# Weight conversion interleaved with the first queries and the first two pairs, in one PSUM rotation

## The chip, the core and the metric

The kernel runs on one core of a Trainium2 chip. Times are device microseconds (us) of one execution; the figure of a kernel is the median of its runs, and less is better.

## What is computed

Attention with a memory, followed by a two-layer feed-forward net, all in float32. Batch 4, 8 heads, 576 tokens, 64 features per head; 2304 tokens in all, 512 features, 2048 hidden features. Of the reference:

```
scores = scale * q @ k^T, causal, softmaxed over keys
local  = a @ v
q_p    = where(q > 0, q, exp(q) - 1) + 1
mem    = (q_p @ M_prev) / (q_p . z_prev + 1e-6)
out    = g * mem + (1 - g) * local          # g = sigmoid(beta), per head
x      = out as (tokens, 512)
h      = x @ w_in
y      = (h * sigmoid(1.702 * h)) @ w_out
```

## The kernel before

Matmuls run on pairs of 32-bit parts: every operand is split in a high part and a low remainder, and three products (high by high, low by high, high by low) are added in PSUM. The weights come as raw 64-bit words. `conv_unit` turns a block of them (128 hidden features) into the two parts in five steps: `load` (a 512 KB transfer into one of two raw buffers `wraw`), `scale` (ScalarE writes `ws` into a PSUM bank), `bits` (three VectorE passes, L177, L178 and L180, the last one giving `wr` and reading both the raw words and `ws`), a copy of the high part `wi` on ScalarE, and the subtraction of the low part on GpSimd. There are 16 blocks of w_in. "Load n" and "conversion n" below are those of the n-th block, in the order in which they are issued.

Attention goes by pairs of heads: pair p is batch p // 4, heads 2 (p % 4) and one more. `plan_prep` places a pair's preparation in numbered slots: `split_hi` on ScalarE, `split_lo_k` and `split_lo_q` on GpSimd, `stack_hi` and `stack_lo` (ten SBUF-to-SBUF transfers, which put high and low parts of keys and queries above each other in `W`), the phi function of the queries and its normalisation. `plan_attend` places the scores (`s_unit`, tiles `ps`), row maxima on VectorE (L483), exponentials on ScalarE (L489), row scaling on GpSimd (L492), transposes (`pt`), their split (`e`) and the products with the values (`po`). Pair p + 1 begins 7 or 8 slots after pair p.

The first 256 tokens of batch 0 are done ahead of that by `first_queries`, all four pairs of heads at once and with their own tiles (`fk`, `fq`, `fa`, ...), so that the first token chunk `x` is there early. `first_moe` is a generator of the matmuls of x @ w_in (tiles `pm`, one block of w_in after another for each chunk of tokens); `step` runs a slot's events and then takes matmuls from this generator up to the slot's share of TensorE time (`PACE`). The results `hk` go out to `gd`. When the attention of a batch is complete (`xd`), its next chunks follow. The second product (tiles `acc`) comes after all of it.

The program's order is a wish list: the framework's scheduler orders each engine's instructions at build time by it, by its own estimate of times, and puts in the waits. On the chip each engine, and the transfer queue of SyncE (SP), issues in that order. A tile from a pool waits for the release of the buffer that it takes over.

PSUM has eight banks: two for `pm`, one for `po`, and five for scores, transposes and conversion: a rotation of four (`ps_s`) and a single one (`ps_x`). The conversions use `ps_x`; after the slot of the last conversion, each fifth tile of attention takes it. All six conversions of the first group (`W0`) are written after `first_queries`, then the loads of pair 0, then the slots from -7 on, with the ten other conversions at the slots of `CONV`.

Of the kernel before, what the change touches and what calls it, by code (L numbers as in the profile page):

```python
# [8 lines left out]
F32 = mybir.dt.float32  # L9
# [25 lines left out]
def tile_attention_memory_moe(ctx, tc, kq, vq, mem, zz, beta, w_in, w_out, out):  # L35
# [5 lines left out]
    PACE = ((20, 2.2), (60, 2.2), (9999, 2.7))  # L41
    LATE = 20
    W0 = 6
    CONV = [-7, -6, -5, -3, -1, 1, 3, 5, 7, 9]
    PSUM = bass.MemoryType.PSUM

    def pool(stack, name, bufs=1, **kw):
        return stack.enter_context(tc.tile_pool(name=name, bufs=bufs, **kw))
# [12 lines left out]
    att = pool(attn, "att", side="right")  # L61
    wkp = pool(attn, "wkp", side="right")
    sml = pool(attn, "sml", 6, side="right")
    ps_s = pool(attn, "ps_s", 4, space=PSUM, side="right")
    ps_x = pool(attn, "ps_x", 1, space=PSUM, side="right")
    ps_o = pool(attn, "ps_o", 1, space=PSUM, side="right")

    xd = [dr.tile([128, NK, S], F32, name=f"xd{b}") for b in range(B)]
# [1 line left out]

    moe_ps = [(ps_m, "pm")]
    events = {}
    state = {"slot": -8, "pe": 0.0, "seq": 0, "sum": 0, "bank": 0}


    def bank(name):
        state["bank"] += 1
        own = state["slot"] > CONV[-1] + 1 and state["bank"] % 5 == 4
        return (ps_x if own else ps_s).tile([128, 512], F32, name=name, tag="ps")

    def at(slot, prio, fn):
        assert slot > state["slot"], (slot, state["slot"])
# [129 lines left out]
    def first_queries(b):  # L212
        K, fsm = [], []
        if b == 0:
            nc.sync.dma_start(gb, beta.to_broadcast([128, H]))
        for c in range(NP):
            t = fst.tile([128, 512], F32, name=f"fk{c}")
            nc.sync.dma_start(t[:, :256], kq[b, c, :, :256])
            nc.sync.dma_start(t[:, 256:], kq[b, c, :, S:S + 256])
            K.append(t)  # L220
        q = fst.tile([128, NP, 2, 128], F32, name="fq")
        nc.sync.dma_start(q, vq[b, :, :, 1, :2].rearrange("c p t d -> p c t d"))
        z = fst.tile([128, NP, 128], F32, name="fz")
        nc.sync.dma_start(z.rearrange("p c d -> p (c d)"), zz[b:b + 1].rearrange("o c d -> o (c d)").to_broadcast([128, NP * 128]))
        v = fst.tile([128, NP, 2, 128], F32, name="fv")
        nc.sync.dma_start(v, vq[b, :, :, 0, :2].rearrange("c p t d -> p c t d"))
        m = fst.tile([128, NP, 128], F32, name="fm")
        nc.sync.dma_start(m, mem[b * NP:b * NP + NP].rearrange("c p h d -> p c (h d)"))
        qm = fst.tile([128, NP * 2, 2, D + 1], F32, name="fqm")
        nc.gpsimd.memset(qm[:, :, :, D:], 1e-6)  # L230
        for c in range(NP):
            fs = fst.tile([128, 2, 2, 2], F32, name="fsm", bufs=NP)
            nc.gpsimd.memset(fs, 1e-9)
            fsm.append(fs)
        box = {}
        aa, fa = {}, {}

        def score(c):
            ps = []
            for h in range(2):  # L240
                r = slice(64 * h, 64 * h + 64)
                p = bank("ps")
                nc.tensor.matmul(p[:, :256], K[c][r, 384:512], K[c][r, :256], start=True, stop=True)
                nc.tensor.matmul(p[:, 256:384], K[c][r, 256:384], K[c][r, :128], start=True, stop=True)
                ps.append(p)
            aa[c] = fst.tile([128, 2, 384], F32, name="fa", bufs=2)
            for h in range(2):
                for i, (o, n) in enumerate(((256, 128), (0, 256))):
                    nm = softmax_max([(ps[h][:, o:o + n], n, mask[:, 512 - n:])])
                    softmax_exp(ps[h][:, o:o + n], aa[c][:, h, o:o + n], nm, fsm[c][:, h, i, :1])  # L250

        def norm(c):
            sm = fst.tile([128, 2, 2], F32, name="fsr", bufs=2)
            nc.vector.tensor_reduce(out=sm, in_=fsm[c], op=ALU.add, axis=AX.X)
            nc.vector.reciprocal(out=sm, in_=sm)
            for h in range(2):
                for i, (o, n) in enumerate(((256, 128), (0, 256))):
                    scale_rows(aa[c][:, h, o:o + n], sm[:, h, i:i + 1], g1[:, 2 * c + h:2 * c + h + 1])
            pt = [bank("pt") for _ in range(2)]
            for h in range(2):  # L260
                nc.tensor.transpose(pt[0][:, 256 * h:256 * h + 128], aa[c][:, h, 256:384], ident)
                nc.tensor.transpose(pt[0][:, 256 * h + 128:256 * h + 256], aa[c][:, h, 0:128], ident)
                nc.tensor.transpose(pt[1][:, 128 * h:128 * h + 128], aa[c][:, h, 128:256], ident)
            fa[c] = fst.tile([128, 768], F32, name="ft", bufs=2)
            copy("A", fa[c][:, :512], pt[0])
            copy("V", fa[c][:, 512:], pt[1][:, :256])

        def phi():
            qv = q.rearrange("p c t (h d) -> p (c t) h d", h=2)
            w = qm[:, :, :, :D]  # L270
            nc.scalar.activation(out=w, in_=qv, func=AF.Relu, scale=-1.0)
            nc.scalar.activation(out=w, in_=w, func=AF.Exp, scale=-1.0)
            nc.vector.scalar_tensor_tensor(out=qv, in0=qv, scalar=0.0, in1=w, op0=ALU.max, op1=ALU.add)
            for c in range(NP):
                tt("P", w[:, 2 * c:2 * c + 2], qv[:, 2 * c:2 * c + 2],
                   z[:, c:c + 1, :].rearrange("p o (h d) -> p o h d", h=2).to_broadcast([128, 2, 2, D]), ALU.mult)
                copy("A", m[:, c], m[:, c], gt[:, c:c + 1])

        def phin():
            n = fst.tile([128, NP, 2, 2, 1], F32, name="fn")  # L280
            nv = n.rearrange("p c t h o -> p (c t) h o")
            nc.vector.tensor_reduce(out=nv[:, :, :, 0], in_=qm, op=ALU.add, axis=AX.X)
            nc.vector.reciprocal(out=n, in_=n)
            for c in range(NP):
                w = q[:, c].rearrange("p t (h d) -> p t h d", h=2)
                tt("P", w, w, n[:, c].to_broadcast([128, 2, 2, D]), ALU.mult)

        def qtr(k):
            if not k:
                box["qt"] = fst.tile([128, NP, 256], F32, name="fqt")  # L290
            qt = box["qt"]
            pt = bank("pt")
            for c in (2 * k, 2 * k + 1):
                for t in range(2):
                    o = 128 * (2 * (c % 2) + t)
                    nc.tensor.transpose(pt[:, o:o + 128], q[:, c, t], ident)
            copy("A", qt[:, 2 * k:2 * k + 2].rearrange("p c q -> p (c q)"), pt)

        def values(c, xl):
            for h in range(2):  # L300
                r = slice(64 * h, 64 * h + 64)
                po = (ps_o if h == 0 else ps_m).tile([128, 512], F32, name="po" if h == 0 else "pm")
                nc.tensor.matmul(po[:, :256], m[:, c], box["qt"][:, c], start=True, stop=False)
                nc.tensor.matmul(po[:, :256], v[:, c, 0], fa[c][:, 256 * h:256 * h + 256], start=False, stop=False)
                nc.tensor.matmul(
                    po[:, 128:256], v[:, c, 1], fa[c][:, 512 + 128 * h:640 + 128 * h], start=False, stop=True)
                copy("A", xq[b][0][r, c, :256], po[r, :256])
                sub("V", xl[r, c, :256], po[r, :256], xq[b][0][r, c, :256])

        if b == 0:  # L310
            gates()
        xl = new_x(b)
        xq[b][0] = mop.tile([128, NK, XW], F32R, name="xh")
        score(0)
        phi()
        score(1)
        norm(0)
        phin()
        score(2)
        norm(1)  # L320
        qtr(0)
        qtr(1)
        values(0, xl)
        score(3)
        norm(2)
        values(1, xl)
        norm(3)
        values(2, xl)
        values(3, xl)

# [397 lines left out]
    NPAIRS = len(pairs)  # L728
    def conv_in(blk):
        wb[blk] = w1[blk >= W0].tile([128, 2, DM], F32R, name=f"wi{blk}")  # L730
        conv_unit(None, wb[blk], w_in[blk], cnv, {"bufs": 2}, lambda: ps_x, {"tag": "ps"}, att, {"tag": f"qpt{blk % 2}", "bufs": 2})

    for b in range(MB):
        first_queries(b)
        xplan[b] = -7
        if b == 0:
            for blk in range(W0):
                conv_in(blk)
    first.close()
    w1.append(pool(left, "w1b", side="left", reuse_waits="tile"))  # L740
    load_kq(0)
    load_vq(0)
    for p in range(NPAIRS):
# [1 line left out]
        plan_attend(p)  # L745
    for blk in range(W0, NB):
        at(CONV[blk - W0], 58, lambda blk=blk: conv_in(blk))
    fill["gen"] = first_moe()
    while state["slot"] < K0[-1] + 16:
        step()  # L750
# [134 lines left out]
```

## Time and profile before

| | us |
|---|---|
| median of 3 runs | 687.38 (687.28 to 688.12) |
| the profiled execution | 689.67 |
| its span, first to last instruction | 687.8 |
| TensorE busy in it | 631.3 |
| VectorE busy | 442.4 |
| ScalarE busy | 406.9 |
| GpSimd busy | 277.9 |

PE is TensorE, DVE VectorE, ACT ScalarE, POOL GpSimd, SPq the queue of SyncE, from which all transfers are issued. PEclk is the granted clock of TensorE as a share of its full speed. In a row of the timeline stand its start, its duration, engine, line, operation, result <- sources, the shape and the count of merged instructions, and in brackets the idle time of the engine ahead of it and what ended it. A transfer's duration there is the time of its issue, not of its bytes.

### The profile page before, as it was taken

What the parts mean: (1) busy time and instruction counts of PE and PEld (TensorE: products, weight loads), DVE (VectorE), ACT (ScalarE), POOL (GpSimd) and SP (SyncE); (2) the same over time, 40 slices, a digit from 0 to 9 for tenths busy, and PEclk for the clock granted to TensorE, in tenths of its full rate; (3) what the DMA queues carried; (4) which work ended last, traced back from release to release, by engine and by line L of the source; (5) the groups of instructions that cost most, each with busy time, mean ns of one, the idle gap of its engine ahead of it and who ended that gap; (6) DMA issues with size and microseconds to landing.
All of it is one profiled execution on the core that took longest, in us unless ns stands there. A gap on an engine that the chain in (4) does not pass through costs nothing.

```text
span 687.8 us, 12522 instructions
## 1 busy us (share of the span) xinstructions
PE 631.3 (92%) x3984; PEld 574.7 (84%) x3984; DVE 442.4 (64%) x1128; ACT 406.9 (59%) x988; POOL 277.9 (40%) x319
## 2 busy tenths in 40 slices
PE   4687788789998799999899998999999999999997
PEld 3476777579986699999899997999888888888897
DVE  3887678857758776687658634826865545555453
ACT  5766478867748785777576534514555445454453
POOL 4967377776637694566485202422500000000000
PEclk9989899999999999999999999999999999999999
DMA  7869548877667666766772127946544335344231
GB/s 257 248 172 276 177 134 233 244 202 189 176 181 195 183 202 186 194 191 172 230 207 77 45 79 262 321 145 229 153 117 133 118 103 157 92 127 134 67 126 55
DMA packets 71427, 116.71 MB, mean 170 GB/s; under 512 B 8769, under 2 KB 41025, under 8 KB 71361
## 3 DMA queue, kind: packets, MB, share of 16 engines
q1 hardware_dynamic: 71360, 115.91, 57.6%
q8 instruction: 32, 0.52, 0.3%
q14 instruction: 35, 0.28, 0.1%
HBM read 63.97 MB, written 27.79 MB: 133 GB/s over the span
## 4 chain that ended last, share of the span: by engine, by line
PE 71%; DMA 8%; DVE 8%; ACT 6%; issue 2%; SPq 2%; POOL 2%; DVEq 0%; ACTq 0%; POOLq 0%
PE acc L89 29%; PE pm L89 25%; PE po L89 6%; PE pt L93 5%; PE ps L89 5%; DMA qr<-in_vq_dram 2%; DMA xl<-xd 2%; DMA kqr<-in_kq_dram 1%; DVE ps L483 1%; DVE e L108 1%; DMA gd<-hk 1%; ACT a L489 1%; ACT hi L98 1%; ACT e L98 1%; DMA wraw<-in_w_in_dram 1%
## 5 line engine op out<-in xcount | busy, mean ns | idle before, releaser
L89 PE MATMUL pm<-xh,wi 128*128 128x288 f32 (+2 forms) x1024 | 224.5, 308 | 15.3 <-ACT hk L98 5.5
L89 PEld LDWEIGHTS pm<-xh,wi 128*128 128x128 f32 x1024 | 170.7, 195 | 19.3 <-ACT hk L98 6.1
L89 PE MATMUL acc<-gh,wo 128*128 128x512 f32 (+1 forms) x640 | 179.3, 368 | 0.0
L89 PE MATMUL pm<-xl,wi 128*128 128x288 f32 (+2 forms) x512 | 155.7, 305 | 0.0
L89 PEld LDWEIGHTS acc<-gh,wo 128*128 128x128 f32 x640 | 115.2, 189 | 19.8
L89 PE MATMUL acc<-gl,wo 128*128 128x512 f32 (+1 forms) x320 | 115.1, 368 | 0.0
L89 PEld LDWEIGHTS pm<-xl,wi 128*128 128x128 f32 x512 | 99.7, 195 | 0.4
L492 POOL TENSOR_SCALAR a<-a,sm,g 128x512 f32<-128x512 f32 (+3 forms) x112 | 71.9, 653 | 65.3 <-DVE sm L531 43.6
L108 DVE TENSOR_TENSOR e<-pt,e 128x320 fp32r<-128x320 f32 (+2 forms) x152 | 70.1, 482 | 39.1 <-ACT e L98 38.3
L785 DVE SCALAR_TENSOR_TENSOR gt<-gt,graw 128x512 f32<-128x512 f32 (+1 forms) x80 | 53.0, 662 | 45.6 <-ACT gt L784 45.1
L483 DVE CUSTOM_DVE_ANT_0 ps<-ps,mask 128x256 f32<-128x256 f32 (+4 forms) x144 | 69.7, 494 | 19.2 <-PE ps L89 14.1
L784 ACT ACTIVATE gt<-graw 128x512 f32<-128x512 f32 (+1 forms) x80 | 47.2, 591 | 55.6 <-DVE gl L108 55.6
L108 DVE TENSOR_TENSOR gl<-gt,gh 128x512 fp32r<-128x512 f32 (+1 forms) x80 | 53.1, 665 | 36.3 <-ACT gh L98 33.2
L489 ACT ACTIVATE a<-ps,nm 128x512 f32<-128x512 f32 (+3 forms) x112 | 60.7, 544 | 26.7 <-DVE nm L483 25.7
L89 PE MATMUL po<-e,vs 128*128 128x320 f32 (+3 forms) x416 | 71.6, 292 | 4.6 <-ACT e L98 4.1
L98 ACT ACTIVATE e<-pt 128x320 fp32r<-128x320 f32 (+2 forms) x152 | 62.2, 436 | 22.4 <-PE po L89 11.5
L98 ACT ACTIVATE gh<-gt 128x512 fp32r<-128x512 f32 (+1 forms) x80 | 47.2, 590 | 41.0 <-PE acc L89 38.6
L89 PEld LDWEIGHTS acc<-gl,wo 128*128 128x128 f32 x320 | 59.4, 189 | 10.1
L89 PEld LDWEIGHTS po<-e,vs 128*128 128x128 f32 x416 | 62.1, 191 | 6.4 <-ACT e L98 4.9
L89 PE MATMUL ps<-W 128*128 128x512 f32 (+3 forms) x224 | 59.9, 350 | 4.4 <-DVE e L108 2.9
L93 PE MATMUL pt<-ident,a 128*128 128x128 f32 x296 | 57.4, 276 | 0.4 <-ACT a L489 0.3
L98 ACT ACTIVATE hk<-pm 128x288 f32<-128x288 f32 (+2 forms) x64 | 26.2, 409 | 53.1 <-PE pm L89 43.7
(125 smaller groups left out, 979.2 us busy)
## 6 DMA issues: line engine op xcount, KB each, us to landing
graw<-gd SPq DMA_DIRECT2D x64, 256.0 KB, 2.7
gd<-hk SPq DMA_DIRECT2D x96, 144.0 KB, 2.6
wraw<-in_w_in_dram SPq DMA_DIRECT2D x16, 512.0 KB, 4.3
wraw<-in_w_out_dram SPq DMA_DIRECT2D x16, 512.0 KB, 5.0
kqr<-in_kq_dram SPq DMA_DIRECT2D x12, 608.0 KB, 5.2
W<-hi SPq DMA_DIRECT2D x24, 272.0 KB, 3.8
W<-loq SPq DMA_DIRECT2D x48, 128.0 KB, 3.7
vr<-in_vq_dram SPq DMA_DIRECT2D x16, 320.0 KB, 4.3
```

The costliest lines, as they stand in the source:

```text
L89: nc.tensor.matmul(out, l, r, start=start, stop=stop)
L93: nc.tensor.transpose(out, in_, idn)
L98: nc.scalar.activation(out=dst, in_=src, func=AF.Copy, **kw)
L108: (nc.vector if eng == "V" else nc.gpsimd).tensor_tensor(out=dst, in0=a, in1=b, op=op)
L483: nc.vector.tensor_tensor_reduce(out=ps, in0=ps, in1=mk, op0=ALU.add, op1=ALU.min, scale=-0.125, scalar=1e38 if j == 0 else nm[:, j - 1:j] ...
L489: nc.scalar.activation(out=a, in_=ps, func=AF.Exp, scale=-1.0, bias=nm, accum_out=sm)
L492: nc.gpsimd.tensor_scalar(out=a, in0=a, scalar1=r, scalar2=gcol, op0=ALU.mult, op1=ALU.mult)
L784: nc.scalar.activation(out=t[:, :n], in_=raw[:, :n], func=AF.Tanh, scale=0.851)
L785: nc.vector.scalar_tensor_tensor(out=t[:, :n], in0=t[:, :n], scalar=1.0, in1=raw[:, :n], op0=ALU.add, op1=ALU.mult)
```

## The change

The loads of pair 0 are issued first and the slots are planned before `first_queries`, which becomes a generator. At each of its first six stops one weight block of the first group is converted, and from the third stop on a slot is run as well, so that four slots (-7 to -4), with pair 0's preparation, lie within the first queries. The ten other conversions stand at slots -3 to 13 rather than -7 to 9. The single bank joins the rotation, which has five banks for scores, transposes and conversions alike.

```
-    CONV = [-7, -6, -5, -3, -1, 1, 3, 5, 7, 9]
+    CONV = [-3, -2, -1, 1, 3, 5, 7, 9, 11, 13]
...
-    ps_s = pool(attn, "ps_s", 4, space=PSUM, side="right")
-    ps_x = pool(attn, "ps_x", 1, space=PSUM, side="right")
+    ps_s = pool(attn, "ps_s", 5, space=PSUM, side="right")
...
     def bank(name):
-        state["bank"] += 1
-        own = state["slot"] > CONV[-1] + 1 and state["bank"] % 5 == 4
-        return (ps_x if own else ps_s).tile([128, 512], F32, name=name, tag="ps")
+        return ps_s.tile([128, 512], F32, name=name, tag="ps")
...
         score(0)
         phi()
+        yield
         score(1)
         norm(0)
         phin()
+        yield
         score(2)
         norm(1)
+        yield
         qtr(0)
         qtr(1)
         values(0, xl)
+        yield
         score(3)
         norm(2)
+        yield
         values(1, xl)
         norm(3)
+        yield
         values(2, xl)
         values(3, xl)
...
-        conv_unit(None, wb[blk], w_in[blk], cnv, {"bufs": 2}, lambda: ps_x, {"tag": "ps"}, att, {"tag": f"qpt{blk % 2}", "bufs": 2})
-
-    for b in range(MB):
-        first_queries(b)
-        xplan[b] = -7
-        if b == 0:
-            for blk in range(W0):
-                conv_in(blk)
-    first.close()
-    w1.append(pool(left, "w1b", side="left", reuse_waits="tile"))
+        conv_unit(None, wb[blk], w_in[blk], cnv, {"bufs": 2}, lambda: ps_s, {"tag": "ps"}, att, {"tag": f"qpt{blk % 2}", "bufs": 2})
+
     load_kq(0)
     load_vq(0)
     for p in range(NPAIRS):
...
     for blk in range(W0, NB):
         at(CONV[blk - W0], 58, lambda blk=blk: conv_in(blk))
+    for k, _ in enumerate(first_queries(0)):
+        conv_in(k)
+        if k >= 2:
+            step()
+    xplan[0] = -7
+    first.close()
+    w1.append(pool(left, "w1b", side="left", reuse_waits="tile"))
     fill["gen"] = first_moe()
```

What the built programs hold, engine by engine, shows the move at three places. A line number of the changed kernel is some four less, or two more, than that of the kernel before; the number behind a tile's name differs between the builds.

On SP at the start of the program, before (`fk`, `fq`, `fz`, `fv`, `fm` belong to the first queries; `kqr`, `vr`, `mr`, `qr`, `zb` to pair 0; `wraw` are raw weights):

```order
L215 DMA gb<-in_beta_dram 128x8
L218 DMA fk_162<-in_kq_dram 128x256
L219 DMA fk_162<-in_kq_dram 128x256
...
L228 DMA fm<-in_mem_dram 128x4x128
L162 DMA wraw<-in_w_in_dram 128x1024 x2
L344 DMA kqr<-in_kq_dram 128x576
L345 DMA kqr<-in_kq_dram 128x384
L353 DMA vr<-in_vq_dram 128x640
```

The same place in the changed kernel:

```order
L346 DMA kqr<-in_kq_dram 128x576
L347 DMA kqr<-in_kq_dram 128x384
L355 DMA vr<-in_vq_dram 128x640
L357 DMA mr<-in_mem_dram 128x128
L360 DMA qr<-in_vq_dram 128x384
L362 DMA zb<-in_zz_dram 128x128
L211 DMA gb<-in_beta_dram 128x8
L214 DMA fk_170<-in_kq_dram 128x256
L215 DMA fk_170<-in_kq_dram 128x256
```

Pair 0's six loads now stand ahead of the first queries' keys and of the first two weight loads.

On PE, where the scores of pair 0 stand (`W_590` and `W_591` in the one, `W_444` and `W_445` in the other), before (`wi_429` is weight block 1):

```order
L89 MATMUL pm<-xh,wi_429 128x256 x2
L89 MATMUL ps<-W_590 128x512 x2
L304 MATMUL pm<-ft,fv 128x256
L305 MATMUL pm<-ft,fv 128x128
L89 MATMUL ps<-W_591 128x512 x2
L303 MATMUL po<-fqt,fm 128x256
```

In the changed kernel (`wi_381` is block 4, `wi_429` block 5 there):

```order
L85 MATMUL pm<-xh,wi_381 128x256 x2
L85 MATMUL pm<-xl,wi_381 128x256
L85 MATMUL ps<-hi 128x288 x2
L85 MATMUL ps<-lok,hi 128x288 x2
L85 MATMUL ps<-hi,loq 128x288 x2
L85 MATMUL ps<-W_444 128x512 x2
L85 MATMUL pm<-xh,wi_429 128x256 x2
```

Pair 0's scores moved from within the first block of chunk 0, and from between the last steps of the first queries, to behind block 4; the last of its scores stand behind block 10.

On SP from load 10 on in the changed kernel (`W_738` and `W_739` are the stacks of pair 1; the `gd` rows are stores of chunk 0's blocks 5 to 8):

```order
L158 DMA wraw<-in_w_in_dram 128x1024
L393 DMA W_738<-hi 64x832
L394 DMA W_738<-hi 64x256
L393 DMA W_739<-hi 64x832
L678 DMA gd_101<-hk 128x256
L394 DMA W_739<-hi 64x256
L399 DMA W_738<-lok 64x576
L678 DMA gd_102<-hk 128x256
L402 DMA W_738<-loq 64x256
L678 DMA gd_103<-hk 128x256
L402 DMA W_738<-loq 64x256
L678 DMA gd_104<-hk 128x256
L399 DMA W_739<-lok 64x576
L402 DMA W_739<-loq 64x256 x2
L158 DMA wraw<-in_w_in_dram 128x1024
```

Before, from load 10 on (`W_1077` and `W_1078` are the stacks of pair 2):

```order
L162 DMA wraw<-in_w_in_dram 128x1024
L400 DMA W_1077<-loq 64x256 x2
L397 DMA W_1078<-lok 64x576
L400 DMA W_1078<-loq 64x256
L676 DMA gd_106<-hk 128x256
L162 DMA wraw<-in_w_in_dram 128x1024
```

Between loads 10 and 11 stood four of pair 2's stack copies and one store before; in the changed kernel all ten of pair 1's and four stores stand there. Between its loads 14 and 15 stand pair 2's last stack copies, two stores and the next keys.

## Rows read from the trace of the kernel before

**Rows 1.** The page: span, and busy time, share and instructions of each engine.

```profile
span 687.8 us, 12522 instructions
PE 631.3 (92%) x3984; PEld 574.7 (84%) x3984; DVE 442.4 (64%) x1128; ACT 406.9 (59%) x988; POOL 277.9 (40%) x319
```

**Rows 2.** Busy time by stretch: length, engines with instructions, PEclk, transfer share, GB/s.

```profile
0.00:50.00 50.00, 33.82 (x156) 26.54 (x156) 33.38 (x102) 33.57 (x88) 33.79 (x66) 0.93 0.74 224
50.00:100.00 50.00, 39.12 (x256) 35.23 (x255) 37.06 (x91) 29.41 (x70) 29.09 (x28) 0.90 0.65 197
100.00:150.00 50.00, 40.72 (x249) 33.02 (x248) 38.25 (x130) 40.86 (x115) 40.57 (x43) 0.97 0.90 243
```

**Rows 3.** Timeline of PE: a block of chunk 0 that waited for its weights.

```profile
88.55 0.42 PE L89 MATMUL pm<-xh,wi 128*128 128x256 f32 x1 [2.14 <-POOL wi L108]
```

**Rows 4.** Busy time by stretch, from 64 to 92 us, columns as in rows 2.

```profile
64.00:92.00 28.00, 20.07 (x119) 18.22 (x118) 20.15 (x44) 13.51 (x32) 14.11 (x13) 0.82 0.62 190
```

**Rows 5.** Timeline of ACT: conversions, the first and last of eight copies.

```profile
64.19 0.63 ACT L98 ACTIVATE wi<-wr 128x512 fp32r<-128x512 f32 x1 [0.69 <-DVE wr L180]
...
73.16 0.62 ACT L98 ACTIVATE wi<-wr 128x512 fp32r<-128x512 f32 x1
73.68 0.62 ACT L170 ACTIVATE ws<-wraw 128x512 f32<-128x512 f32 x1
...
92.40 0.62 ACT L98 ACTIVATE wi<-wr 128x512 fp32r<-128x512 f32 x1
```

**Rows 6.** Timeline of DVE: the passes of one conversion.

```profile
74.33 0.70 DVE L177 TENSOR_SCALAR ws<-ws 128x512 int32<-128x512 int32 x1 [1.46 <-ACT ws L170]
75.07 0.70 DVE L178 SCALAR_TENSOR_TENSOR ws<-wraw,ws 128x512 int32<-128x512 int32 x1
75.87 0.69 DVE L180 SCALAR_TENSOR_TENSOR wr<-wraw,ws 128x512 int32<-128x512 int32 x1
```

**Rows 7.** Issues with median us to landing: 0 to 50, 50 to 64, 64 to 92 us.

```profile
wraw<-in_w_in_dram SPq DMA_DIRECT2D x8, 512.0 KB, 4.3
...
wraw<-in_w_in_dram SPq DMA_DIRECT2D x2, 512.0 KB, 5.7
...
wraw<-in_w_in_dram SPq DMA_DIRECT2D x6, 512.0 KB, 3.6
```

**Rows 8.** Timeline of SP: first issue, some loads of w_in, stack copies, a store.

```profile
0.74 0.39 SPq L215 DMA_DIRECT2D gb<-in_beta_dram  x1
...
7.01 1.71 SPq L162 DMA_DIRECT2D wraw<-in_w_in_dram  x2
...
21.78 0.54 SPq L162 DMA_DIRECT2D wraw<-in_w_in_dram  x1
...
46.23 1.19 SPq L400 DMA_DIRECT2D W<-loq  x2
...
50.83 0.34 SPq L676 DMA_DIRECT2D gd<-hk  x1
...
61.08 0.60 SPq L162 DMA_DIRECT2D wraw<-in_w_in_dram  x1
...
64.89 0.38 SPq L162 DMA_DIRECT2D wraw<-in_w_in_dram  x1
...
80.56 0.33 SPq L162 DMA_DIRECT2D wraw<-in_w_in_dram  x1
...
85.24 0.33 SPq L162 DMA_DIRECT2D wraw<-in_w_in_dram  x1
```

**Rows 9.** Timeline of PE: first scores; first 512-column scores of pairs 2 and 3.

```profile
4.30 1.23 PE L243 MATMUL ps<-fk 64*128 64x256 f32 x4 [4.30 <-DMA fk<-in_kq_dram]
...
93.14 0.72 PE L89 MATMUL ps<-W 128*128 128x512 f32 x2
...
106.86 0.72 PE L89 MATMUL ps<-W 128*128 128x512 f32 x2
```

**Rows 10.** Timeline of DVE: row maximum of pair 2's first scores.

```profile
93.90 0.70 DVE L483 CUSTOM_DVE_ANT_0 ps<-ps,mask 128x512 f32<-128x512 f32 x1 [0.38 <-PE ps L89]
```

More of the change, by code (lines that the diff above doesn't have):

```diff
@@ L72, in tile_attention_memory_moe @@
     events = {}
-    state = {"slot": -8, "pe": 0.0, "seq": 0, "sum": 0, "bank": 0}
+    state = {"slot": -8, "pe": 0.0, "seq": 0, "sum": 0}
     def bank(name):
-        state["bank"] += 1
-        own = state["slot"] > CONV[-1] + 1 and state["bank"] % 5 == 4
-        return (ps_x if own else ps_s).tile([128, 512], F32, name=name, tag="ps")
+        return ps_s.tile([128, 512], F32, name=name, tag="ps")
     def at(slot, prio, fn):
```

## The prediction, made before the changed kernel was run

> **What bounds the kernel now.** I read the page first. The profiled execution took 689.67 us, 1.9 us more than its span of 687.8 us, in which TensorE is busy 631.3 us [rows 1]. Its idle time, 56.5 us, is all that a new order can win, as the change leaves the number of matmuls as it is. The busy times by stretch say where it lies [rows 2]: 16.2 us in the first 50 us, 10.9 in the second, 9.3 in the third: 36.4 of the 56.5. No other engine is full there (VectorE 33.4, 37.1 and 38.3 of 50 us), so the front waits along chains. The change touches this front.
>
> The order of TensorE's waits then shows two kinds. Up to 50 us it waits for the steps of the first queries. From 64 to 92 us it waits for weights: its blocks of token chunk 0 start only when VectorE, ScalarE and GpSimd have converted their block of w_in, the longest time 2.14 us [rows 3], and in these 28 us it works 20.07 us, at a granted clock of 0.82 [rows 4]. One conversion there has a fixed round. ScalarE copies the high part (`wi`, at 73.16) and at once scales the next block (`ws`, 0.52 later); VectorE, idle for 1.46 us until then, makes its three passes, which end at 76.56, and the next `wi` follows [rows 5, 6]. Eight such copies from 64.19 to 92.40 us come 4.0 us apart [rows 5]. The single bank `ps_x` makes this round: the next scale waits until the third pass has read it.
>
> Third, the queue. SP issues all loads in order. The sixteen loads of w_in leave between 7.01 and 85.24 us [rows 8]; one lands 3.6 to 5.7 us after its issue, by the traffic around it [rows 7]. Two raw buffers exist, so a load leaves only after the third pass of the block two before.
>
> From the first 512-column scores of pair 2, at 93.14 us, the rest goes by pairs: those of pair 3 stand at 106.86, 13.7 us on [rows 9]. Of chunk 0 only the last block is left behind the first of these marks. The next chunk of tokens takes up its matmuls inside pair 5 in both orders, and everything later hangs behind that. So I forecast the time of one mark, the scores of pair 2, and carry its shift 1:1 to the end.
>
> **The change part by part.** No engine gains or loses an instruction that matters: this is order, queues and banks alone.
>
> *Pair 0's loads go first.* Six transfers (1.12 MB by their shapes) leave ahead of the first queries' keys. Lower bound of the delay: six issues at 0.48 us (thirteen from 0.74 to 7.01 [rows 8]), 2.9 us. Upper bound: 1.12 MB at the 224 GB/s of the stretch [rows 2], 5.0 us. I take 3.7, in the middle since some keys travel together with them: first score at 8.0 us, not 4.30 [rows 9]. In return, pair 0's splitting, phi and stacking run in the empty first 10 us.
>
> *Conversions come between the steps of the first queries.* On ScalarE the first scale now stands ahead of the exponentials of the second score, and each copy waits for VectorE while the exponentials behind it wait too. The two first weight loads end with all the early bytes, at about 18 us, so conversion 1 is through at about 21 us and load 3 leaves then (21.78 before: even). Load 3's scale stands behind four exponentials, a weight copy and pair 1's `vs` and `ms`; its passes end at 32.4. Load 5 leaves then, lands 4.3 us later [rows 7], and its scale, 0.62, and three passes, 3 x 0.70 with row maxima between them, end at 40.6 [rows 5, 6]. Load 7 leaves at 40.6 and lands at 44.9. Conversions 6 and 7 stand pass by pass beside each other on VectorE: with load 7's scale done at 45.5, the first pass of 7, both second and both third passes and a copy between them end at 48.9 (6) and 49.7 (7). So loads 8 and 9 leave at 49.0 and 49.8. Load 8 lands 3.6 us later, its scale ends at 53.2, and three passes with two small copies of results and a pass of 9 between them end at 55.8: load 10 leaves at 56 (61.08 before [rows 8]). The first queries end at about 50 us in both orders. Up to here the change is ahead by one conversion and 5 us of loads, and behind by pair 0's scores and softmax, which before were done by 50 us and now stand behind four blocks of chunk 0.
>
> *The loads behind pair 1's stacking.* Now ten stack copies of pair 1 and four stores of chunk 0's results stand on SP between loads 10 and 11. A copy takes 0.6 us of the queue (1.19 for two) and a store 0.34 [rows 8]: 7.4 us of issue alone. They can't begin before ScalarE has split pair 1's keys, an instruction that stands behind the weight copy of conversion 8: 57.3 us by my walk. Three copies go at once; the four stores wait for the results of blocks 5 to 8, which I put at 59.8, 61.1, 62.4 and 63.9, and the last three copies follow. I get 66.3 us for load 11, bounds 64.7 (issue alone) and 68 (the blocks half a round later); 64.89 before [rows 8]. The lead of 5 us is gone. The buffer would have been free at 58.4: the wait is the queue's, so the shared rotation, which frees the next scale from the bank, helps no conversion from 11 on. Load 13 then leaves at 74.4 (one round of 4.5 + 0.62 + 2.1 and qp later).
>
> *The loads behind pair 2's stacking.* Loads 15 and 16 stand behind the same ten copies of pair 2 and two stores. Its keys are split at 76.8 and its low parts done at 79.7 on GpSimd; one store waits for block 12, at 85.7. Load 15 leaves at 87.3, load 16 at 88.9, against 80.56 and 85.24 [rows 8]. Landing 3.7, a scale behind exponentials, and the passes put block 15's high part at 96.0 us.
>
> *The mark.* In the changed order TensorE does one matmul of block 15 before pair 2's scores, so these start at about 96.2 us, not 93.14: +3.1. The last passes of conversions 15 and 16 now stand on VectorE ahead of the row maximum of these scores, which began at 93.90 [rows 10] and which I put at 97.9. So +4.0 us. Behind the mark I count nothing: what hides chunk 0's last block is pair 2's own round (13.7 us long, of which TensorE needs about half), and without that cover it would cost its 1.5 us of matmuls.
>
> *TensorE's clock.* From 64 to 92 us the clock is 0.82 of full (a mix of the 1.2 and 2.4 GHz levels) after gaps as the one of 2.14 us [rows 3, 4]. The changed order has blocks 2 to 4 of chunk 0 in one piece, 36 matmuls. If that kept the clock full, the 20.07 us would be up to 3.6 us shorter. I give it no credit, as the engine waits for weights there. The Trainium skill ("TensorE: Matmul & The Clock Gate", Loop structure matters more than you think) recommends just such an unbroken stretch of matmuls; taken as the measure, it would put the sum at about no change, the third rival below. The row speaks against it: a faster matmul only lengthens the wait that follows.
>
> **The sum.** +4.0 us on the median of 687.38 (the profiled run is 2.3 us above it; I shift both alike): 691.4 us.
>
> **The rivals.** *Slower, as summed*: 691.4, of its own 689 to 696. *Faster*: the free rotation sets the pace. If pair 1's split comes early enough that the stack copies are out of SP's way before load 11's buffer is free (by 58.4 us; the stack then has to begin by 51), conversions run at their buffers' round, half of 4.3 + 0.62 + 2.1 plus a wait, 3.7 us each. Conversion 10 ends at 64 and 15 at 82.5; then the pairs set the pace: two rounds of 13.7 us behind pair 0's scores, at 60 to 61.5 by my walk, put the mark at 87.4 to 88.9. I take 4 us earlier: 683.4. For it speaks that load 10 is early; against it that split stands behind the copy of conversion 8. *No change*: the clock as above gives 3.6 of the 4.0 us back: 687.8. *Far slower*: loads land as at 50 to 64 us, 5.7 us rather than 4.3 [rows 7], in the five rounds that stand on the path (5, 7, 8, 11, 15); 5 x 1.4 = 7 us more: 698.
>
> **How the numbers follow.** Within 0.2% is 686.0 to 688.8 us, which is about what a measurement can tell. Slower as summed 0.52, far slower 0.08, no change 0.14, faster 0.26. The forecast is the likeliest, 691.4. The walk adds some hundred waits by hand, and both bounds of load 11 and of the first delay move it by 2 us each; the range of 8 in 10 goes from 683.0, just past the faster case, to 698.0, just the far slower one.
>
> **What would show it.** First score at 7.5 to 9 us; load 10 at 55 to 58; load 11 held behind stack copies until 64.7 or later, with its buffer free before; load 15 after 85; pair 2's 512-column scores at 95 to 99, and about 13.7 us to pair 3's. It is wrong if load 11 leaves before 62 (the queue didn't hold it), if the mark is before 93, or if the mark is late and the end isn't (a give-back in pairs 2 to 5).

## The result: 0.8% slower

The changed kernel takes 694.79 us (median; 693.29 to 696.96), the kernel before 687.75 in the same comparison. The ratio is 1.0080, with a 95% interval of 1.0052 to 1.0107. Of 687.38 us that is +5.5 us (3.6 to 7.4); the forecast was +4.0. The two medians alone lie 7.0 us apart, inside that interval; with four runs a side, and those of the kernel before between 687.28 and 691.26, the size is known no better than that. The profiled execution took 693.29 us; from its page, the span and the busy line [rows 1]:

```profile
span 691.5 us, 12536 instructions
PE 625.2 (90%) x3984; PEld 570.6 (83%) x3984; DVE 440.9 (64%) x1128; ACT 406.4 (59%) x988; POOL 275.0 (40%) x319
```

TensorE is idle for 66.3 us, not 56.5: +9.8. The busy times by stretch (start and end, length, then each engine's busy time and count, the granted clock, the share of transfers and GB/s) say where [rows 2]:

```profile
0.00:50.00 50.00, 24.61 (x109) 19.37 (x110) 29.28 (x80) 28.60 (x72) 29.32 (x62) 1.00 0.67 203
50.00:100.00 50.00, 39.25 (x258) 35.17 (x256) 36.81 (x94) 28.83 (x70) 26.88 (x28) 0.90 0.70 205
100.00:150.00 50.00, 38.55 (x246) 33.70 (x247) 39.18 (x129) 39.97 (x108) 37.15 (x35) 0.93 0.76 199
```

Of this, 9.2 us are lost in the first 50 us: 24.61 us busy there against 33.82 before, and 109 matmuls instead of 156. The next stretch, with 39.25 us, is level with before (39.12); the third, with 38.55 against 40.72, adds 2.2 us. So the deficit isn't made good by 150 us. Which waits make it, the waits of TensorE up to 50 us tell (what waits, for what: us in total, times, longest). First the kernel before:

```profile
PE pt L261 <- POOL fa L492: 5.1, 2, 3.5
PE ps L243 <- DMA fk<-in_kq_dram: 4.3, 1, 4.3
PE pm L303 <- DVE xl L108: 3.8, 1, 3.8
PE pt L296 <- POOL fq L108: 2.5, 1, 2.5
```

Then the changed kernel:

```profile
PE ps L239 <- DMA fk<-in_kq_dram: 8.8, 1, 8.8
PE pt L257 <- POOL fa L494: 6.9, 2, 5.4
PE ps L239 <- ACT ft L94: 6.0, 1, 6.0
PE pt L292 <- ACT fa L491: 3.5, 1, 3.5
```

The head costs 4.5 us more. A wait of 6.0 us is new: a *score* (`ps`) of the first queries waits for ScalarE. What it waits for is `ft`, the copy that empties a bank of transposes; on ScalarE that copy stands at 24.91 us, right behind the first weight copy (23.82) and the second scale (24.36):

```profile
24.91 0.58 ACT L94 ACTIVATE ft<-pt 128x512 f32<-128x512 f32 x1
```

The score and the marks of pairs 2 and 3 (their first 512-column scores) stand in TensorE's timeline [rows 9]:

```profile
25.54 1.25 PE L239 MATMUL ps<-fk 64*128 64x256 f32 x3 [6.02 <-ACT ft L94]
...
103.21 1.06 PE L85 MATMUL ps<-W 128*128 128x512 f32 x2
...
115.51 0.71 PE L85 MATMUL ps<-W 128*128 128x512 f32 x2
```

The third score of the first queries stood at 12.94 us before, and stands at 25.54; chunk 0's first matmul moved from 42.56 to 48.16. The mark is 10.1 us late (93.14 before), that of pair 3 8.7 us (106.86).

The queue of SP at load 3, between loads 10 and 11, and at load 15 [rows 8]:

```profile
26.48 0.36 SPq L158 DMA_DIRECT2D wraw<-in_w_in_dram  x1
...
60.56 0.38 SPq L158 DMA_DIRECT2D wraw<-in_w_in_dram  x1
62.11 0.47 SPq L393 DMA_DIRECT2D W<-hi  x1
...
65.68 0.46 SPq L399 DMA_DIRECT2D W<-lok  x1
66.26 0.51 SPq L678 DMA_DIRECT2D gd<-hk  x1
...
70.24 1.23 SPq L402 DMA_DIRECT2D W<-loq  x2
71.51 0.58 SPq L158 DMA_DIRECT2D wraw<-in_w_in_dram  x1
...
92.10 0.43 SPq L158 DMA_DIRECT2D wraw<-in_w_in_dram  x1
```

The third passes of conversions 1 and 9 on VectorE, which free the buffers of loads 3 and 11 [rows 6]:

```profile
23.11 0.68 DVE L176 SCALAR_TENSOR_TENSOR wr<-wraw,ws 128x512 int32<-128x512 int32 x1
...
62.06 0.69 DVE L176 SCALAR_TENSOR_TENSOR wr<-wraw,ws 128x512 int32<-128x512 int32 x1
```

And ScalarE's timeline, with the first scale, that of load 15 and the last weight copy of w_in [rows 5]:

```profile
20.90 0.63 ACT L166 ACTIVATE ws<-wraw 128x512 f32<-128x512 f32 x1 [0.96 <-DMA wraw<-in_w_in_dram]
...
97.15 0.63 ACT L166 ACTIVATE ws<-wraw 128x512 f32<-128x512 f32 x1 [1.68 <-DMA wraw<-in_w_in_dram]
...
105.27 0.62 ACT L94 ACTIVATE wi<-wr 128x512 fp32r<-128x512 f32 x1
```

The stack copies and stores do stand between loads 10 and 11, which leave 10.95 us apart. Load 11's buffer was free at 62.75 us, so the queue held it for 8.8 us; loads 12 and 15 left 6.0 and 6.2 us after their buffers were free. The tenth weight copy is level with before (68.07 against 68.90 us); the sixteenth is 12.9 us late (92.40 before).

### The profile page after: what moved, and what is told of

Its sections match the earlier page's. It is cut to its first block, busy times and chain, and to the rows that moved or that the text cites. A ratio compares the mean times of both kernels' runs of the same rounds, so it can differ in the third digit from the quotient of the medians.

```text
span 691.5 us, 12536 instructions
## 1 busy us (share of the span) xinstructions
PE 625.2 (90%) x3984; PEld 570.6 (83%) x3984; DVE 440.9 (64%) x1128; ACT 406.4 (59%) x988; POOL 275.0 (40%) x319
## 4 chain that ended last, share of the span: by engine, by line
PE 67%; DMA 14%; ACT 7%; SPq 3%; issue 3%; POOL 2%; DVE 2%; ACTq 0%; POOLq 0%; DVEq 0%
PE acc L85 29%; PE pm L85 23%; PE po L85 5%; PE pt L89 5%; DMA wraw<-in_w_in_dram 4%; PE ps L85 4%; DMA xl<-xd 3%; DMA kqr<-in_kq_dram 1%; DMA qr<-in_vq_dram 1%; ACT a L491 1%; ACT e L94 1%; DMA gd<-hk 1%; DMA xd<-xf 1%; SPq L402 1%; DMA vr<-in_vq_dram 1%
## 5 line engine op out<-in xcount | busy, mean ns | idle before, releaser
L85 PE MATMUL pm<-xh,wi 128*128 128x288 f32 (+2 forms) x1024 | 219.6, 303 | 9.8 <-DVE hk L97 3.4
L85 PEld LDWEIGHTS pm<-xh,wi 128*128 128x128 f32 x1024 | 167.1, 191 | 14.3 <-DVE hk L97 4.1
L85 PE MATMUL pm<-xl,wi 128*128 128x288 f32 (+2 forms) x512 | 153.5, 301 | 0.4 <-DVE xl L104 0.4
L85 PEld LDWEIGHTS pm<-xl,wi 128*128 128x128 f32 x512 | 97.7, 191 | 1.1 <-DVE xl L104 0.6
L786 DVE SCALAR_TENSOR_TENSOR gt<-gt,graw 128x512 f32<-128x512 f32 (+1 forms) x80 | 51.5, 644 | 45.4 <-ACT gt L785 45.0
L97 DVE COPY hk<-pm 128x288 f32<-128x288 f32 (+2 forms) x64 | 29.1, 454 | 44.6 <-PE pm L85 31.2
```

The costliest lines, as they stand in the source:

```text
L85: nc.tensor.matmul(out, l, r, start=start, stop=stop)
L97: nc.vector.tensor_copy(dst, src)
L786: nc.vector.scalar_tensor_tensor(out=t[:, :n], in0=t[:, :n], scalar=1.0, in1=raw[:, :n], op0=ALU.add, op1=ALU.mult)
```

## The experiments

In all runs the matmuls are the same 3984. The ratio of the changed kernel is that of the result; each other ratio is to the kernel before, run anew on the same chip (medians 690.1 to 690.6 us, single runs 685.3 to 695.1). "Last copy" is the sixteenth weight copy of w_in, "mark" the first 512-column score of pair 2, both from the profile.

| kernel | ratio | interval | last copy | mark |
|---|---|---|---|---|
| before | 1 | | 92.40 | 93.14 |
| changed | 1.0080 | 1.0052 to 1.0107 | 105.27 | 103.21 |
| changed, pair 0's loads later | 1.0075 | 1.0047 to 1.0103 | 103.56 | 100.27 |
| changed, weights ahead of them too | 1.0102 | 1.0067 to 1.0138 | 106.92 | 104.79 |
| before, pair 0's loads first | 1.0033 | 1.0010 to 1.0056 | 98.24 | 98.64 |
| changed, weight loads from ScalarE | 1.0054 | 1.0026 to 1.0081 | 100.63 | 99.48 |
| before, weight loads from ScalarE | 1.0019 | 0.9986 to 1.0051 | 93.33 | 94.46 |
| before, rotation alone | 1.0099 | 1.0063 to 1.0134 | 103.09 | 108.53 |
| changed, old banks | 1.0111 | 1.0077 to 1.0146 | 105.08 | 90.17 |
| the same, not interleaved | 1.0126 | 1.0084 to 1.0168 | 107.53 | 91.36 |
| the same, old slots | 1.0078 | 1.0052 to 1.0104 | 101.67 | 102.07 |
| before, new slots alone | 1.0030 | 0.9999 to 1.0060 | 100.14 | 83.66 |
| changed, slots after first queries | 1.0155 | 1.0120 to 1.0191 | 107.21 | 105.62 |
| three remedies together | 1.0137 | 1.0099 to 1.0175 | 97.02 | 102.89 |

### The head of the queue, three ways

Pair 0's loads behind those of the first queries:

```
-    load_kq(0)
-    load_vq(0)
     for p in range(NPAIRS):
...
     for k, _ in enumerate(first_queries(0)):
+        if k == 0:
+            load_kq(0)
+            load_vq(0)
         conv_in(k)
```

> The changed kernel, with pair 0's six loads issued behind those of the first queries. Theory (head and queue: the late first score and SP's holds of the weight loads make the loss): the first score stands at 4.3 to 5 us again, the first weight scale 3 to 5 us earlier than 20.90, pair 2's 512-column scores at 96 to 100 instead of 103.2, and the time is 689 to 692 us, about half of the loss given back. Rival (the conversions between the steps of the first queries cost the time on ScalarE and VectorE, whatever comes first): the mark stays at 102 to 104 us and the time at 693 to 696.

The first score stood at 4.40 us, as expected, and the first scale at 19.70 instead of 20.90 (3 to 5 us earlier was expected). The mark, at 100.27, hardly missed the range; the time didn't move. TensorE's third score in that run:

```profile
24.80 1.22 PE L239 MATMUL ps<-fk 64*128 64x256 f32 x2 [11.71 <-DVE wr L176]
```

The 4.4 us won at the head became part of a longer wait. The first two weight loads now leave behind pair 0's, at 14.60 us, and the row shows that the score needs a bank that the first conversion frees only with its third pass (`wr`). The next run gives these two loads their place ahead of pair 0's (the two calls stand behind `conv_in(1)`, at `k == 1`):

> The changed kernel, with pair 0's six loads behind the first queries' loads and behind the first two loads of w_in, so that the head of SP's queue is that of before. Theory C (what costs is the head of the queue: in the run with loads later, the first two loads of w_in left at 14.60 us instead of 7.01, and the next score waited 11.7 us for the bank of the first conversion): first score at 4.3, first two weight loads at 7.0, first scale at 17 or before, 125 or more matmuls by 50 us, and a ratio to the kernel before of 0.999 to 1.004. Theory B (interleaving on ScalarE and VectorE costs the front whatever the head is): 105 to 120 matmuls by 50 us, ratio 1.005 to 1.010.

The head was that of before (first score 4.32, weight loads 7.02, first scale 16.88), and nothing was won: 100 matmuls by 50 us, ratio 1.0102. The third score again:

```profile
22.00 1.22 PE L239 MATMUL ps<-fk 64*128 64x256 f32 x2 [8.98 <-DVE ft L97]
```

Theory C falls for the changed kernel: in there the head isn't what the front waits for. Theory B comes nearer, though both numbers lie just beyond its ranges (105 to 120 matmuls, 1.005 to 1.010); and the row names the banks as much as the engines' order, here a bank of transposes that VectorE's copy `ft` empties. The same six loads alone, in the kernel before:

```
+    load_kq(0)
+    load_vq(0)
     for b in range(MB):
         first_queries(b)
...
-    load_kq(0)
-    load_vq(0)
     for p in range(NPAIRS):
```

> The kernel before, with pair 0's six loads first and nothing else. Theory C: first score at 8 to 9 us, first two weight loads 3 us or more later than 7.01, first weight copy 3 to 5 us later than 22.16, and a ratio of 1.004 to 1.007, the delay of the head carried to the end. Rival (a delay of the head is swallowed by the waits for weights from 64 to 92 us): 0.998 to 1.002.

```profile
8.75 0.80 PE L243 MATMUL ps<-fk 64*128 64x256 f32 x2 [8.75 <-DMA fk<-in_kq_dram]
...
10.66 2.15 SPq L162 DMA_DIRECT2D wraw<-in_w_in_dram  x2
...
98.24 0.63 ACT L98 ACTIVATE wi<-wr 128x512 fp32r<-128x512 f32 x1 [1.17 <-DVE wr L180]
```

The head 4.5 us later, the last copy 5.8 us, the end 0.33% or 2.3 us (0.7 to 3.8). Carried, but to about half; a little below what theory C expected.

### The loads taken out of SP's queue

Loads 3 to 16 are issued by ScalarE, each behind the weight copy of the block two before it, whose buffer it takes over:

```
+    def raw_in(blk, eng):
+        raw = early[blk] = cnv.tile([128, DM, 2], I32, name="wraw", bufs=2)
+        eng.dma_start(raw.rearrange("p f w -> p (f w)"), w_in[blk].bitcast(I32))
...
+        if blk + 2 < NB:
+            raw_in(blk + 2, nc.scalar)
```

> The changed kernel, with the loads of w_in from the third on issued by ScalarE, each right behind the weight copy that frees its buffer, so that none stands behind stack copies, stores or unfinished transfers of SP. Theory (SP's queue holds loads 3, 5, 11, 15 and 16): load 3 leaves by 24.5 us, load 11 by 65, load 15 by 88, pair 2's 512-column scores stand at 92 to 98 us and the time is 685 to 690. Rival (ScalarE's and VectorE's own order holds the conversions, the queue only follows): loads leave earlier and their scales wait, the mark stays at 101 to 104, the time at 692 to 696.

Load 3 left at 25.28, later than expected; 11 and 15 left within the expected bounds. From ScalarE's queue and timeline (loads 11 and 15, last copy), and the mark:

```profile
61.31 0.36 ACTq L738 DMA_DIRECT2D wraw<-in_w_in_dram  x1
...
84.91 0.33 ACTq L738 DMA_DIRECT2D wraw<-in_w_in_dram  x1
...
100.63 0.61 ACT L94 ACTIVATE wi<-wr 128x512 fp32r<-128x512 f32 x1
...
99.48 1.05 PE L85 MATMUL ps<-W 128*128 128x512 f32 x2
```

Load 11 is 10.2 us earlier, load 15 7.2, the last copy 4.6, the mark 3.7: more than a third of the mark's delay was the queue's, less than half. The ratio, 1.0054, is lower by 0.26 points, but the two intervals overlap: a gain in time isn't shown. Both theories missed; the truth lies between. In the kernel before the same edit should show whether its queue holds loads too:

> The kernel before, with the loads of w_in from the third on issued by ScalarE right behind the weight copy that frees their buffer. Queue theory of the forecast (SP's queue holds loads in the kernel before too): block 15's copy 3 us or more earlier than 88.79, ratio 0.992 to 0.997. Rival (there the passes of one conversion set the round, as the single bank makes it): copies within 2 us of before, ratio 0.998 to 1.003.

The last copy came at 93.33 and the ratio is 1.0019, so nothing was to be had there: the rival's numbers.

### The rotation

The kernel before, with five shared banks and nothing else:

```
-    ps_s = pool(attn, "ps_s", 4, space=PSUM, side="right")
-    ps_x = pool(attn, "ps_x", 1, space=PSUM, side="right")
+    ps_s = pool(attn, "ps_s", 5, space=PSUM, side="right")
...
-        conv_unit(None, wb[blk], w_in[blk], cnv, {"bufs": 2}, lambda: ps_x, {"tag": "ps"}, att, {"tag": f"qpt{blk % 2}", "bufs": 2})
+        conv_unit(None, wb[blk], w_in[blk], cnv, {"bufs": 2}, lambda: ps_s, {"tag": "ps"}, att, {"tag": f"qpt{blk % 2}", "bufs": 2})
```

> The kernel before, with the shared rotation of five banks alone (the scales take their bank from it); order, slots and queue as before. Theory: the raw buffers and the queue set the rounds, so the mark stays at 92 to 94 us and the time within 1.5 us of the kernel before (686 to 689). Rival (the rotation is what costs: scales and scores wait for one another's banks): mark at 97 or later, time 691 or more. Other rival (the single bank set the rounds of 4.0 us): load 15 leaves 3 us or more earlier than 80.56 us, the mark at 89 to 91, time 683 to 685.

```profile
34.48 0.63 ACT L167 ACTIVATE ws<-wraw 128x512 f32<-128x512 f32 x1
```

That is the first scale, at 16.47 us before. In a shared rotation a tile takes its bank in the order in which the program is written, and there all conversions are written behind the first queries' scores and transposes: so the first scale waits for those (told from the program's order; the row itself names no releaser). Without the interleaving the rotation costs. Now the changed kernel with the old banks:

> The changed kernel with the old banks: the scales take the one bank of their own again, four banks stay for scores; interleaving, slots and pair 0's early loads as changed. Theory A (the shared rotation: a score of the first queries waits for the bank that a weight conversion holds, and the conversion for its load): the second score of the first queries stands 5 us or more earlier, TensorE runs 125 matmuls or more by 50 us (109 in the changed kernel, 158 before), pair 1's split comes before 50 us, ratio to the kernel before 0.995 to 1.003. Theory B (the interleaved program order on ScalarE and VectorE): 105 to 120 matmuls by 50 us, ratio 1.005 to 1.010.

```profile
28.66 1.23 PE L242 MATMUL ps<-fk 64*128 64x256 f32 x4
...
90.17 0.63 PE L88 MATMUL ps<-W 128*128 128x512 f32 x2
...
105.08 0.63 ACT L97 ACTIVATE wi<-wr 128x512 fp32r<-128x512 f32 x1 [1.43 <-DVE wr L179]
```

The third and fourth scores of the first queries came at 19.46 and 28.66 us (25.54 and 40.62 in the changed kernel), TensorE ran 131 matmuls by 50 us (109, and 156 before), and pair 1 was split at 44.80 (61.09): all as theory A had it. The mark was even earlier than before. But the time was not: 1.0111. So the rotation does cause the new wait of the first queries, but the end gained nothing from its going. What did not move is the last weight copy, at 105.08. And here SP's queue is not what makes it late. The pass that frees load 11's buffer, and load 11:

```profile
70.96 0.68 DVE L179 SCALAR_TENSOR_TENSOR wr<-wraw,ws 128x512 int32<-128x512 int32 x1
...
72.83 0.38 SPq L161 DMA_DIRECT2D wraw<-in_w_in_dram  x1
```

The load left 1.2 us after the end of that pass, and from load 10 on none left more than 1.4 us after its buffer was free. From the seventh copy (61.71) on the copies come 4.8 us apart; which of the passes' own waits makes that round was not tried. So a last copy as late as the changed kernel's, and a time no better, come without loads held by the queue too.

TensorE's clock differs as well. The busy times from 64 to 92 us, first of the changed kernel, then of this run:

```profile
64.00:92.00 28.00, 21.44 (x133) 19.10 (x132) 18.68 (x53) 16.21 (x43) 17.40 (x18) 0.82 0.78 217
...
64.00:92.00 28.00, 22.07 (x158) 19.41 (x156) 22.12 (x55) 18.08 (x43) 15.17 (x14) 0.99 0.71 213
```

### Interleaving, slots, and pair 0's slots

From the run with the old banks, the six conversions put behind the first queries again:

```
     for k, _ in enumerate(first_queries(0)):
-        conv_in(k)
         if k >= 2:
             step()
     xplan[0] = -7
+    for k in range(W0):
+        conv_in(k)
```

> As the run with the old banks, and the six first conversions written behind the first queries again, as before; so pair 0's loads and preparation ahead of and within the first queries, and the later slots, are what is left of the change. Theory A: within 0.3% of the run with the old banks. Theory B: 0.4% or more below it, ratio 0.993 to 1.002. Head theory of the forecast (pair 0's loads ahead delay all by 4 us): ratio 1.004 to 1.008 with the first score at 8 to 9 us.

1.0126, last copy 107.53: no difference that the intervals show, as theory A had it: with the old banks the interleaving shows no cost. Here too the loads from 10 on left within 1.6 us of their buffers' release. From it, the old slots:

> As the run without interleaving, with the later conversions at the slots of before, as far as these are still ahead (-3 for the first four, then -1 to 9). What is left of the change is pair 0's loads and preparation. If the later slots cost time (weights 15 and 16 come behind pair 1's work), the ratio is 0.3% or more below the run without interleaving and block 15's copy 4 us or more earlier; if the loads set the conversions, within 0.2% and 2 us.

```profile
24.43 0.91 SPq L161 DMA_DIRECT2D wraw<-in_w_in_dram  x2
...
101.67 0.63 ACT L97 ACTIVATE wi<-wr 128x512 fp32r<-128x512 f32 x1 [1.22 <-DVE wr L179]
```

Last copy 5.9 us earlier (block 15's 3.7, where 4 or more was expected), ratio lower by 0.48 points, though the intervals overlap. Without interleaving the first weight loads stand behind pair 0's stack copies and leave at 24.43 us. The slots alone, in the kernel before (`CONV` as changed):

> The kernel before with the changed table of slots alone (-3 to 13 instead of -7 to 9). If the slots cost time by themselves: the copies of blocks 12 to 15 come 4 us or more later than 73.16 to 88.79, pair 2's results later than 121.23, ratio 1.004 to 1.010. If the loads and VectorE's order set the pace: ratio 0.998 to 1.003.

```profile
83.66 0.74 PE L89 MATMUL ps<-W 128*128 128x512 f32 x2
...
100.14 0.63 ACT L98 ACTIVATE wi<-wr 128x512 fp32r<-128x512 f32 x1 [1.43 <-DVE wr L180]
```

The last copy is 7.7 us later; pair 3's split (82.14 us; 96.71 before) and what hangs on it now stand ahead of the last conversions, which is the likely reason. The mark is 9.5 us *earlier*, and the kernel is not faster: 1.0030. The last four slots of pair 0 moved out of the first queries again (the two lines with `step()` left out of the loop):

> The changed kernel, without running slots inside the first queries: conversions 0 to 5 and pair 0's loads stay where they are, but pair 0's split, stacking and phi follow the first queries. Theory (the stack copies of pair 0 on SP, each waiting for the transfer eight before it, hold loads 3 and 5): load 3 leaves at 22 to 24.5 us instead of 26.48, load 5 by 35; the first queries end 2 to 4 us earlier; the mark at 98 to 102 and the time 690 to 693. Rival (pair 0's preparation inside the first queries is worth its place): pair 0's first 512-column scores move from 60 us to 64 or later, the mark to 105 or later, the time to 695 or more.

1.0155: slower than the changed kernel, as the rival had it. The expected reason is wrong, though, so this run does not show what the slots are worth there. The scheduler kept pair 0's split at 5.54 us and its first 512-column score at 59.20; load 3 left at 25.30 and chunk 0 began 1.1 us earlier. The loss came from 100 to 125 us (108 matmuls at a granted clock of 0.79; 139 at 0.93 in the changed kernel); what made it I did not find.

### The remedies together

The head of before, loads from ScalarE and slots of -3, -3, -2, -1, 0, 1, 3, 5, 7, 9 in the changed kernel:

> The changed kernel with the head of the queue of before, the later weight loads on ScalarE's queue, and slots of -3, -3, -2, -1, 0, 1, 3, 5, 7, 9: the three remedies together. If head, queue and slots are what costs in the change, and their parts add (the earlier runs: 0.3 per cent for the queue, 0.3 to 0.5 for the slots, and the head), the ratio is 0.990 to 0.998. If the interleaving itself costs, it stays at 1.002 or above.

The last copy came at 97.02 us, 8.3 us earlier than in the changed kernel, and the ratio was 1.0137: the parts don't add. Pair 0's first 512-column score slid to 68.19 us. No version beat the kernel before.

## Why the prediction was right, and where its sizes were off

- *Direction and kind.* Slower: right. That weights are held by the queue is right too, and shown twice, by the rows between loads 10 and 11, and by the run that takes the loads out of that queue. That the kernel is slower *because* of it is not shown: that run's gain lies within the intervals, and the run with the old banks loses as much though its queue holds no load from 10 on by more than 1.4 us. Of the forecast's own signs load 10 (55 to 58 us) and the mark (95 to 99) missed.
- *"First score at 8.0 us"*: 8.83. Alone this is worth 2.3 us at the end, shown by the kernel before with pair 0's loads first. Within the changed kernel the two runs that win it back show no gain; a later wait swallows it.
- *"Load 3 leaves then (21.78 before: even)"*: it left at 26.48. Two terms were mis-sized here, each by about half of the 5.5 us. The first two weight loads were put at about 18 us, and the first scale, which waits for its load, began at 20.90; so conversion 1 freed its buffer at 23.79 and not at about 21 (loads landed in 5.4 us, the median of those issued up to 50 us, not 4.3). And "in return, pair 0's splitting, phi and stacking run in the empty first 10 us" costed its ten stack copies on SP at nothing. They stood there from 12.92 to 25.25 us, five of them waiting for the transfer eight places ahead (rows below), and load 3 left 2.7 us after its buffer was free. The later loads are late by about as much: loads 10, 11, 13 and 15 were forecast at 56, 66.3, 74.4 and 87.3 and left at 60.56, 71.51, 78.59 and 92.10, +4.2 to +5.2. The hold itself was sized well: 10.3 us between loads 10 and 11 forecast, 10.95 measured, though 8.8 of these were the queue's (66.3 against 58.4, so 7.9, were forecast).
- *"The first queries end at about 50 us in both orders"*: chunk 0 began 5.6 us later, and the last of the first queries' products stands at 52.66 us. The walk followed ScalarE and VectorE, and not the banks: the 6.02 us wait of the third score was missing. I had looked at what the shared rotation gives the scales, not at what the scales take from the scores. The run with the old banks shows that it is real, and that its going alone did not help the end.
- *"The loads behind pair 1's stacking ... the rotation helps no conversion from 11 on"*: the queue is only part. With the loads out of it the last copy is still 8.2 us late, about what the new slots alone cost (7.7). That the last conversions stand behind the work of more pairs on ScalarE and VectorE too, and not on SP alone, fits both runs, but was not tried apart.
- *"Carry its shift 1:1 to the end"*: failed. The mark was 10.1 us late and the end 5.5 (3.6 to 7.4). The two errors, a mark 7.0 us later than forecast and a carry of about half, cancelled: that +4.0 came so near to +5.5 is luck. As a gauge the mark was badly chosen: three runs had it earlier than before and were not faster. The last weight copy goes better with the time, over all kernels of the table but the last row at 0.6 us of time for one of copy; that is a correlation, and the last row stands off it: a copy 4.6 us late, and 9.5 us of time.
- *The clock.* I gave no credit, and from 64 to 92 us it was 0.82 again [rows 4]. In the run with the old banks it was 0.99 there, and that kernel is no faster (1.0111): a fuller clock in this stretch did not decide the time. The Trainium skill's advice of long unbroken stretches ("TensorE: Matmul & The Clock Gate", Loop structure matters more than you think) had been the case for no change; the changed kernel shows no gain from it in that stretch.
- *The faster rival* had what it asked of the queue in the run with loads from ScalarE (load 11 at 61.31, as its buffer came free), and the conversions still did not run at their buffers' round: from the tenth copy to the sixteenth they came 5.0 us apart, not 3.7.

What stays open: the cause of the loss as a whole, and how the parts combine. Head and slots alone cost 0.33 and 0.30%, and the rotation alone 0.99%, while the whole costs 0.80%. Each run also makes the scheduler order the rest anew, up to the end, so that a difference of two runs is never one edit alone.

## What to carry to other kernels

Two users of one rotation take turns in written order: before merging buffers, ask what each new user makes the old ones wait for, and whether the order of the program is the order in which you want them. Where a wait at the head of a chain is removed, look for the next wait behind the same bank or queue before counting the gain. And gauge a front by the last thing that later work needs (here, as far as a correlation goes, the last weights), not by a milestone that a new order can move by itself.

## What the runs showed unexpectedly

SP's transfers wait for one another. The waits of its queue in the changed kernel from 12 to 26 us:

```profile
SPq L399 <- DMA wraw<-in_w_in_dram: 2.1, 1, 2.1
SPq L402 <- DMA wraw<-in_w_in_dram: 1.7, 1, 1.7
SPq L394 <- DMA fz<-in_zz_dram: 1.3, 1, 1.3
SPq L399 <- DMA fv<-in_vq_dram: 1.0, 1, 1.0
SPq L402 <- DMA fm<-in_mem_dram: 0.4, 1, 0.4
```

No stack copy uses `fz`, `fv`, `fm` or `wraw`: each of these is the transfer eight places ahead in the queue, whose landing the built program awaits before it issues the copy. So here the short copies behind long loads moved at the pace of the loads: 6.5 us of waiting for five copies.

TensorE's busy time, for the same 3984 matmuls, was 624.0 to 625.9 us in the changed kernel and its variants with pair 0's loads later, weights ahead, and loads from ScalarE, and 629.4 to 634.0 in the ten others. Some 6 us of the idle time of the changed kernel are given back in this way; the mean granted clock (0.968 to 0.987 in the four, 0.956 to 0.983 in the others) does not sort them. Why is open.
